# Gating the first unit alone and forming the decay between superchunks on GpSimd, in a GateLoop and GEGLU kernel

## The chip, the cores and the metric

The kernel runs on one core of a Trainium2 chip. The metric is the time of one execution on the device, in microseconds (us). Each kernel was run several times beside runs of the kernel before on the same chip. The detailed numbers come from one profiled execution of each kernel; its span is about 2 us shorter than the time that is measured for the same execution, so spans are compared with spans and times with times. A run more than 1.5% above the fastest of its kernel is called slow; ratios, their intervals and the verdicts (faster or slower from 2% on) use the other runs alone, the fast ones.

Engines in the profile: PE is TensorE (matmul), PEld its weight loads, DVE is VectorE, ACT is ScalarE, POOL is GpSimd, SP is SyncE. L239 is line 239 of that kernel's file, so the same statement can have another number in another kernel.

## The reference

A gated linear recurrence feeds a gated feed-forward layer. Sizes are 4 batches, 8 heads, 768 steps, head size 48; the second part has 3072 tokens, width 384, inner width 1536.

```python
# recurrence, for each batch and head; a is complex and |a| is capped at 0.999
for t in range(S):
    S_re, S_im = a_re*S_re - a_im*S_im + k[t] (x) v[t],  a_re*S_im + a_im*S_re
    y[t] = q[t] @ S_re
# then, on the tokens
gelu(x @ w_gate) * (x @ w_val) @ w_out      # ffn
out = x + sigmoid(x @ w_res) * ffn
```

## The kernel before

The sequence is cut into superchunks ("groups" g) of 256 steps, three to a batch. Two groups make a unit, and there are six units, 0 to 5. A unit goes through two kinds of stage:

- its gate: from `a` the log magnitude `lm` and the angle `th`; their running sums by matmul (`csl`, `cst`); `E` and `Ei`, the exponential of the sum and its inverse; an arctan; the reduction of the angle `r`, `fg`; and `CS`, the sine and cosine;
- its expert stage: the attention of the unit, with the feed-forward matmuls `gp`, `vp` and their Gelu, while the next unit's products and attention start beside it.

The first `CS` of a unit waits for the last `fg` of a group; the first Gelu of a unit comes right behind the gate of the next unit, behind a load of ScalarE's table. So the first Gelu marks the end of a gate.

The state `G` of the recurrence goes from one group to the next. It is multiplied by the decay `M` of a whole group, a product of three rows: the last row of `E` of the group before, the first row of `Ei` and the exponential of the first row of `lm`. `M` is needed with head size on partitions, and the rows have it along the free axis, so each decay goes through DRAM: rows out, then read back with another pattern (`turn`). Groups 1, 2, 4, 5, 7, 8, 10 and 11 need one: units 0, 1, 3 and 4 have one each, units 2 and 5 two each.

```python
def cs_t(g, c):                       # ... cut: angle sums into cs3 by matmul
    r = pS.tile([128, H, D], FP, tag="r", name="r")          # pS has 2 buffers of a tag
    nc.vector.tensor_scalar(out=r, in0=cs3, scalar1=MAGIC, ...)
    nc.vector.tensor_tensor(out=fg[:, hs, 1, :], in0=cs3, in1=r, op=OP.subtract)
    if c == C - 1:
        nc.vector.scalar_tensor_tensor(out=fg[:, :, 0, :], ...)       # the last fg of a group

def turn(nm, g, srcs):                # rows to DRAM (md), then back, turned (m)
    for i, src in enumerate(srcs):
        nc.gpsimd.dma_start(out=md[i:i + 1, :], in_=src)
    for u in range(2):
        nc.gpsimd.dma_start(out=m[u * D:(u + 1) * D]..., in_=md.rearrange("r (h d) -> d (r h)", h=H))
# decay0: turn the row of lm     decay1: ScalarE takes its exp, once turned
# decay2: turn the rows of E, Ei
def decay3(g):                        # two small products on VectorE
    nc.vector.tensor_tensor(out=M[0:DD], in0=m[0:DD, 0], in1=m[0:DD, 1], op=OP.mult)
    nc.vector.tensor_tensor(out=M[0:DD], in0=M[0:DD], in1=T["m1", g][0:DD, 0], op=OP.mult)

def enter():                          # in attention(g, 0), g not the first of its batch
    # s == 1:  G = dk * M        s == 2:  G = (dk + G) * M      on VectorE, then a cast to Gb

def phase_x(u):                       # gate of unit u+1, first half of the gate of u+2
    # ... cut
    weave((0.0, 0.12, csls), ..., (0.01, 0.01, dec1), (0.46, 0.46, dec),
          (0.2, 0.65, cst), (0.7, 0.95, atn + sin), (0.95, 0.95, dec3), ...)
```

`weave` gives the order in the program text. The order of instructions on each engine is then set when the kernel is compiled, by a scheduler that may move an instruction forward, and each engine runs its instructions in that order. Loads of `a`, `q`, `k` and the stores are issued on SyncE; `v`, the weights and the decay rows on GpSimd. `after_landing(t, f)` places the loads of `f` behind a small GpSimd copy of tile `t`.

Of the kernel before, what the change touches and what calls it, by code (L numbers as in the profile page):

```python
# [9 lines left out]
FP = mybir.dt.float32  # L10
BF = mybir.dt.bfloat16
AF = mybir.ActivationFunctionType
OP = mybir.AluOpType
# [3 lines left out]
def weave(*streams):  # L17

    order = []
    for si, (begin, end, steps) in enumerate(streams):  # L20
        n = len(steps)
        for i, step in enumerate(steps):
            order.append((begin + (end - begin) * (i + 0.5) / n, si, i, step))
    for _, _, _, step in sorted(order, key=lambda e: e[:3]):
        step()
# [3 lines left out]
def kernel(  # L29
# [13 lines left out]
    nc = tc.nc  # L43
    B, H, S, D = q.shape
    DD = 2 * D
    DM = H * D
# [3 lines left out]
    C = 2  # L50
    W = C * DM
    NS = S // (128 * C)
# [38 lines left out]
    pS = ctx.enter_context(tc.tile_pool(name="pS", bufs=2))  # L91
# [5 lines left out]
    mp = ctx.enter_context(tc.tile_pool(name="mp", bufs=3))  # L97
# [4 lines left out]
    dr = ctx.enter_context(tc.tile_pool(name="dr", bufs=2, space=bass.MemoryType.DRAM))  # L102
# [6 lines left out]
    T = {}  # L109
    order = mybir.DependencyInfo(mybir.DependencyClass.NoSync, mybir.DependencyReason.DATA)  # L110

    def tab(ins):

        if "tab" in T:
            tc.add_manual_dep(ins.ins, T["tab"].ins.name, order, reason="table order")
        T["tab"] = ins

    def act(**kw):
        tab(nc.scalar.activation(**kw))  # L119

    def rows(a, g, c):
        b, s = divmod(g, NS)
        t0 = (s * C + c) * 128
        return a[b, :, t0:t0 + 128, :].rearrange("h t d -> t h d")
# [9 lines left out]
    def load_q(g):  # L134
        for nm, src in (("q", q), ("k", k)):
            t = ldq.tile([128, C, H, D], FP, tag=nm, name=nm)
            for c in range(C):
                nc.sync.dma_start(out=t[:, c], in_=rows(src, g, c))
            T[nm, g] = t
        t = ldv.tile([128, C, H, D], BF, tag="v", name="v")  # L140
        for c in range(C):
            nc.gpsimd.dma_start(out=t[:, c], in_=rows(v, g, c))  # L142
        T["v", g] = t
# [15 lines left out]
    def after_landing(t, f):  # L159

        w = singles.tile([1, 1], FP, name="landed%d" % len(T))
        i = nc.gpsimd.tensor_copy(out=w, in_=t[0:1, C - 1, H - 1, D - 1:D])
        with tc.issue_after(i.ins):
            f()

    def flat(t):
        return t.rearrange("p c h d -> p (c h d)")


    def p1_steps(g):  # L170

        def s0():
            T["lm", g] = flat(T["ar", g])
            T["th", g] = flat(T["ai", g])
            act(out=T["lm", g], in_=T["lm", g], func=AF.Ln)

        def s1():
            T["s", g] = pS.tile([128, W], FP, tag="s", name="s")
            act(out=T["s", g], in_=T["lm", g], func=AF.Exp, scale=-1.0)
            nc.vector.tensor_tensor(out=T["th", g], in0=T["s", g], in1=T["th", g], op=OP.mult)  # L180

        def s2():
            act(out=T["s", g], in_=T["th", g], func=AF.Square)

        def s3():
            act(out=T["s", g], in_=T["s", g], func=AF.Ln, bias=1.0)
            lm = T["lm", g]
            nc.vector.scalar_tensor_tensor(out=lm, in0=T["s", g], scalar=0.5, in1=lm, op0=OP.mult, op1=OP.add)
            nc.vector.tensor_scalar(out=lm, in0=lm, scalar1=LNMAX, scalar2=None, op0=OP.min)  # L189

        return [s0, s1, s2, s3]
# [54 lines left out]



    def turn(nm, g, srcs):
        n = len(srcs)  # L250
        md = dr.tile([n, DM], FP, tag="d" + nm, name="d" + nm)
        for i, src in enumerate(srcs):
            nc.gpsimd.dma_start(out=md[i:i + 1, :], in_=src)
        m = mp.tile([128, n, H], FP, tag=nm, name=nm)
        for u in range(2):
            nc.gpsimd.dma_start(out=m[u * D:(u + 1) * D].rearrange("p r h -> p (r h)"),
                                in_=md.rearrange("r (h d) -> d (r h)", h=H))
        T[nm, g] = m

    def decay0(g):  # L260
        turn("m1", g, [T["lm", g][0:1, 0:DM]])

    def decay1(g):
        m = T["m1", g]
        act(out=m[0:DD], in_=m[0:DD], func=AF.Exp)

    def decay2(g):
        turn("m2", g, [T["E", g - 1][127:128, DM:W], T["Ei", g][0:1, 0:DM]])

    def decay3(g):  # L270
        m = T["m2", g]
        M = mp.tile([128, H], FP, tag="M", name="M")
        nc.vector.tensor_tensor(out=M[0:DD], in0=m[0:DD, 0], in1=m[0:DD, 1], op=OP.mult)
        nc.vector.tensor_tensor(out=M[0:DD], in0=M[0:DD], in1=T["m1", g][0:DD, 0], op=OP.mult)
        T["M", g] = M

    def products(g):
# [152 lines left out]
    def op_step(u, jj):  # L430
        h2 = T["h2", u]
        ps = psM.tile([128, DM], FP, tag="mm", padded_shape=[128, 512], name="op")
        for ffi in range(KF):
            nc.tensor.matmul(out=ps, lhsT=h2[:, ffi, jj * 128:(jj + 1) * 128], rhs=wo[:, ffi, :],  # L434
                             start=(ffi == 0), stop=(ffi == KF - 1))
        ot = ob.tile([128, DM], FP, tag="ot", name="ot")
        nc.vector.scalar_tensor_tensor(out=ot, in0=T["sg", u][:, jj], scalar=1.0, in1=ps, op0=OP.add, op1=OP.mult)  # L437
        nc.vector.tensor_tensor(out=ot, in0=ot, in1=T["x", u * 4 + jj], op=OP.add)
        t0 = (u * 4 + jj) * 128
        nc.sync.dma_start(out=out[t0:t0 + 128, :], in_=ot)  # L440


    def table(nm):
        def f():
            tab(nc.scalar.preload_act_table_set(nm))  # L445
        return f

    def gs(u):
        return [2 * u, 2 * u + 1] if 0 <= u < NU else []

    def call(f, *a):
        return lambda: f(*a)

    def zip_steps(lists):
        return [st[i] for i in range(max(map(len, lists), default=0)) for st in lists if i < len(st)]
# [12 lines left out]
    def phase_x(u):  # L468

        pend = []  # L470
        g1, g2 = gs(u + 1), gs(u + 2)
        d1 = [g for g in g1 if g % NS > 0]
        d2 = [g for g in g2 if g % NS > 0]
        ops = [call(op_step, u - 1, jj) for jj in range(4)] if 0 <= u - 1 < NU else []
        att = att_steps(u, 1)
        if not g1:
            weave((0.0, 0.8, att), (0.1, 1.0, ops))
            return

        def csl(g, c):  # L480
            pend.append(cs_l(g, c))

        def ex():
            pend.pop(0)()

        def p1(g):
            return p1_steps(g) + ([call(decay0, g)] if g % NS > 0 else [])
        csls = [call(csl, g, c) for g in g1 for c in range(C)]
        exs = [ex for _ in g1 for _ in range(C)]
        dec = [call(decay2, g) for g in d1]  # L490
        atn = [table("trig_and_small")] + [call(p1_arctan, g) for g in g2]
        cst = [call(carry, g) for g in g1] + [call(cs_t, g, c) for g in g1 for c in range(C)]
        sin = [call(p2_sin, g) for g in g1]
        dec1 = [call(decay1, g) for g in d1]
        dec3 = [call(decay3, g) for g in d1]
        table("natural_log_exp_and_others")()
        if u < 0:

            for f in [st for g in g1 for st in p1(g)] + csls + exs + dec + zip_steps([p1(g) for g in g2]) + dec1:
                f()  # L500
            for f in atn[:1] + [call(p1_arctan, g) for g in g1] + cst + sin + atn[1:] + dec3:
                f()
            return
        weave((0.0, 0.12, csls), (0.05, 0.5, zip_steps([p1(g) for g in g2])), (0.01, 0.01, dec1), (0.12, 0.45, exs),
              (0.46, 0.46, dec), (0.2, 0.65, cst), (0.7, 0.95, atn + sin), (0.95, 0.95, dec3), (0.0, 0.8, att), (0.1, 1.0, ops))

    def phase_y(u):

# [5 lines left out]
        pr = [st for g in gs(u + 1) for st in products(g)]  # L514
        weave((0.0, 1.0, gv), (0.0, 0.4, pr), (0.3, 0.95, att_steps(u + 1, 0)))

    for g in gs(0) + gs(1):
        load_a(g)
    for g in gs(0):
        load_q(g)  # L520
    after_landing(T["k", 0], load_w_in)
    for u in range(-1, NU + 1):
        phase_x(u)
        for g in gs(u + 3):
            load_a(g)
        if u == -1:
            for g in gs(1):
                load_q(g)
            after_landing(T["k", 2], load_w_out)
        phase_y(u)  # L530
        for g in gs(u + 3):
            load_q(g)


# [28 lines left out]
```

## Time and profile before

| | kernel before |
|---|---|
| time, median of 3 runs | 344.1 us (342.87 to 363.25; the longest is a slow run; a fourth run was made beside the kernel after) |
| span of the profiled run | 341.4 us |
| first CS of unit 0 | 45.46 us |
| arctan of unit 1 | 86.15 us |
| first CS of unit 1 | 88.54 us |
| decay M of unit 1 ready | 92.38 us |
| first Gelu of units 0, 1, 2, 3, 4, 5 | 95.90, 142.08, 188.52, 235.82, 279.84, 312.81 us |

Three rows of the page of the kernel before, in 40 slices of 8.5 us; a digit is a share in tenths. PE is TensorE's busy share, PEclk the granted clock, DMA the share of the DMA engines.

```profile
PE   0330544298689979899897999779999989999995
PEclk9996585559699999999999999999999999999999
DMA  9999999999999999527422620021000210002002
```

There are two regimes. Up to slice 11, about 95 us, TensorE is often idle, and its granted clock (the share of full speed that it was allowed) is at 0.5 to 0.8 in seven of the eleven slices. After that TensorE is nearly full in every second stage.

ScalarE's timeline of the kernel before (start, duration, engine, line, operation, tiles, and in brackets the idle time before it and what ended it):

```profile
45.46 0.94 ACT L119 ACTIVATE CS<-fg,hpi 128x768 bf16<-128x768 f32 x1 [7.29 <-DVE fg L237]
...
64.32 0.21 ACT L119 ACTIVATE m_268<-m_268 96x8 f32<-96x8 f32 x1 [8.90 <-DMA m_268<-dm_266]
...
86.15 1.58 ACT L119 ACTIVATE ai<-ai 128x768 f32<-128x768 f32 x2
...
88.54 0.94 ACT L119 ACTIVATE CS<-fg,hpi 128x768 bf16<-128x768 f32 x1 [0.45 <-DVE fg L237]
...
95.90 1.08 ACT L119 ACTIVATE h_776<-gp 128x512 bf16<-128x512 f32 x2
```

The chain of waits of the kernel before, the pieces of the decay (start, duration, what):

```profile
44.80 13.88 DMA dm_266<-ar
...
59.62 4.62 DMA m_268<-dm_266
...
76.31 8.40 DMA dm_663<-Ei
...
85.89 4.42 DMA m_666<-dm_663
```

A row of 1.5 KB took 13.9 us to land, and ScalarE stood 8.9 us for the turned row (`m_268`). VectorE's timeline at the end of unit 1's gate shows where the decay stood:

```profile
87.56 0.94 DVE L237 SCALAR_TENSOR_TENSOR fg<-fg 128x768 f32<-128x768 f32 x1
...
90.40 0.16 DVE L273 TENSOR_TENSOR M<-m_666 96x8 f32<-96x8 f32 x1 [0.23 <-DMA m_666<-dm_663]
...
91.35 0.95 DVE L237 SCALAR_TENSOR_TENSOR fg<-fg 128x768 f32<-128x768 f32 x1
92.22 0.16 DVE L274 TENSOR_TENSOR M<-M,m_268 96x8 f32<-96x8 f32 x1
...
93.17 0.55 DVE L344 TENSOR_TENSOR G<-G,M 96x384 f32<-96x384 f32 x1
```

The last `fg` of the gate (91.35) comes before the second product of `M` and before `G <- M`. The decay became ready late, and hardly any of the gate waited for it. Its last input (`m_666`) had landed at 90.31 us; the second product of `M` then stood behind other work of VectorE.

### The profile page before, as it was taken

The page shows a single profiled execution, that of the slowest core. Times are in us where ns is not written, and L with a number is a line of the kernel's source. Part 1 is how long each engine was busy: PE and PEld are TensorE (multiplying, and loading weights), DVE is VectorE, ACT ScalarE, POOL GpSimd, SP SyncE. Part 2 cuts the span into 40 slices and gives each one's busy share as a digit, 9 for nine tenths or more (in the row PEclk, how much of TensorE's full clock was granted, in tenths as well). Part 3 has the DMA queues.
Part 4 walks back from the last instruction along what each step waited for, and adds up shares of the span by engine and source line. Part 5 has one row for each costly group of instructions (what it writes and reads, how often), then busy time and mean ns, then how long its engine had stood idle before and what let it go on. Part 6 is the DMA issues. An engine that isn't in the chain of part 4 may idle for free.

```text
span 341.4 us, 5552 instructions
## 1 busy us (share of the span) xinstructions
PE 267.3 (78%) x2054; PEld 160.6 (47%) x2080; DVE 245.4 (72%) x440; ACT 203.0 (59%) x338; POOL 67.1 (20%) x104
## 2 busy tenths in 40 slices
PE   0330544298689979899897999779999989999995
PEld 0110224275256545465554566445665556565452
DVE  1322696249999649999389998499994799855443
ACT  3365434349665696756896656977568275662530
POOL 9423710050522224102232000150001300000000
PEclk9996585559699999999999999999999999999999
DMA  9999999999999999527422620021000210002002
GB/s 139 136 139 175 176 184 196 175 170 171 155 167 162 169 133 172 109 46 72 25 63 54 118 46 2 2 48 47 3 2 1 50 46 2 0 2 92 2 1 92
DMA packets 135258, 30.25 MB, mean 89 GB/s; under 512 B 127168, under 2 KB 135232, under 8 KB 135232
## 3 DMA queue, kind: packets, MB, share of 16 engines
q1 hardware_dynamic: 103296, 23.60, 40.6%
q0 software_dynamic: 31936, 6.31, 21.9%
q8 instruction: 16, 0.26, 0.3%
q14 instruction: 10, 0.08, 0.1%
HBM read 31.33 MB, written 4.76 MB: 106 GB/s over the span
## 4 chain that ended last, share of the span: by engine, by line
PE 47%; DMA 18%; DVE 15%; ACT 9%; issue 7%; POOL 3%; ACTq 0%; DVEq 0%; POOLq 0%
PE vp L414 12%; PE gp L410 11%; PE op L434 6%; DMA dm_266<-ar 4%; DMA v<-in_v_dram 4%; PE tp L320 3%; PE at L327 3%; PE tp L317 3%; PE rp L426 3%; DMA dm_663<-Ei 2%; ACT L445 2%; DVE fg L237 2%; DVE r L234 2%; DMA dm_219<-ar 2%; ACT CS L119 2%
## 5 line engine op out<-in xcount | busy, mean ns | idle before, releaser
L410 PE MATMUL gp<-xT,wg 128*128 128x512 bf16 x196 | 61.5, 382 | 7.6 <-DVE xT L401 4.6
L414 PE MATMUL vp<-xT,wv 128*128 128x512 bf16 x210 | 60.3, 382 | 0.3
L322 ACT COPY qk<-tp 96x512 bf16<-96x512 bf16 x48 | 27.9, 581 | 28.3 <-PE tp L320 15.1
L180 DVE TENSOR_TENSOR ai<-s,ai 128x768 f32<-128x768 f32 x12 | 11.1, 955 | 38.5 <-ACT s L119 26.9
L330 DVE TENSOR_TENSOR atm<-at,mask_81 128x512 bf16<-128x512 f32 x48 | 32.8, 683 | 7.2 <-PE at L327 7.2
L410 PEld LDWEIGHTS <-wg 128*128 128x128 bf16 x216 | 20.0, 98 | 23.0 <-issue 8.9
L317 PE MATMUL tp<-ident,Q 128*96 128x128 bf16 x192 | 20.1, 231 | 13.4 <-DVE qk L323 8.6
L142 POOL DMA_DIRECT2D v<-in_v_dram x24 | 21.3, 902 | 43.0 <-PE y L367 22.4
L414 PEld LDWEIGHTS <-wv 128*128 128x128 bf16 x216 | 20.4, 98 | 19.3 <-issue 0.8
L317 PEld LDWEIGHTS <-Q 128*96 128x96 bf16 x192 | 17.3, 131 | 21.4 <-issue 10.0
L323 DVE COPY qk<-tp 96x512 bf16<-96x512 bf16 x48 | 19.9, 414 | 10.1 <-ACT qk L322 9.6
L203 PE MATMUL csl<-ar,lt0a 128*128 128x384 f32 x24 | 12.3, 601 | 18.6 <-DVE ar L189 18.5
L119 ACT ACTIVATE CS<-fg,hpi 128x768 bf16<-128x768 f32 x12 | 11.2, 935 | 24.1 <-DVE fg L237 24.1
L445 ACT ACT_TABLE_LOAD x18 | 23.1, 1283 | 1.0 <-PEq L547 0.7
L320 PE MATMUL tp<-ident,K 128*96 128x128 bf16 x192 | 22.1, 235 | 0.0
L227 PE MATMUL cst<-ai,lt0b 128*128 128x384 f32 x24 | 11.6, 568 | 13.4 <-ACT ai L119 13.1
L327 PE MATMUL at<-qk 96*128 96x128 bf16 x192 | 20.4, 228 | 0.1
L437 DVE SCALAR_TENSOR_TENSOR ot<-sg,op 128x384 f32<-128x384 f32 x24 | 13.2, 549 | 9.4 <-PE op L434 9.4
L365 PE MATMUL y<-v,atm 128*128 128x48 bf16 x192 | 17.9, 187 | 2.5 <-DVE atm L330 2.4
L365 PEld LDWEIGHTS <-atm 128*128 128x128 bf16 x192 | 13.5, 98 | 12.8 <-DVE atm L330 11.6
L320 PEld LDWEIGHTS <-K 128*96 128x96 bf16 x192 | 17.3, 133 | 0.0
L357 PEld LDWEIGHTS <-K 128*96 128x96 bf16 x160 | 13.3, 138 | 6.5 <-DVE K L292 4.2
(155 smaller groups left out, 626.3 us busy)
## 6 DMA issues: line engine op xcount, KB each, us to landing
ar<-in_a_re_dram SPq DMA_DIRECT2D x24, 192.0 KB, 5.7
ai<-in_a_im_dram SPq DMA_DIRECT2D x24, 192.0 KB, 5.5
q<-in_q_dram SPq DMA_DIRECT2D x24, 192.0 KB, 5.1
k<-in_k_dram SPq DMA_DIRECT2D x24, 192.0 KB, 5.0
out_dram<-ot SPq DMA_DIRECT2D x24, 192.0 KB, 1.9
v<-in_v_dram POOLq DMA_DIRECT2D x24, 96.0 KB, 6.3
wg<-in_moe_w_gate_dram POOLq DMA_DIRECT2D x4, 288.0 KB, 9.2
wv<-in_moe_w_val_dram POOLq DMA_DIRECT2D x4, 288.0 KB, 10.5
```

The source lines that it names most:

```text
L142: nc.gpsimd.dma_start(out=t[:, c], in_=rows(v, g, c))
L317: nc.tensor.transpose(out=tp[0:DD, j * 128:j * 128 + 128], in_=Q(x), identity=ident)
L320: nc.tensor.transpose(out=tp[0:DD, 512 + j * 128:640 + j * 128], in_=K(x), identity=ident)
L322: nc.scalar.copy(out=qk[0:DD, 0:512], in_=tp[0:DD, 0:512])
L323: nc.vector.tensor_copy(out=qk[0:DD, 512:1024], in_=tp[0:DD, 512:1024])
L327: nc.tensor.matmul(out=at[:, j], lhsT=qk[0:DD, 512 + j * 128:640 + j * 128], rhs=qk[0:DD, j * 128:j * 128 + 128], start=True, stop=True)
L330: nc.vector.tensor_tensor(out=atm, in0=at, in1=mask4, op=OP.mult)
L365: nc.tensor.matmul(out=ys, lhsT=st["atm", hg][:, j], rhs=V(h), start=True, stop=first)
L410: nc.tensor.matmul(out=gp, lhsT=wg[:, fi, ffi * 128:(ffi + 1) * 128], rhs=xT[:, fi, :], start=(fi == 0), stop=(fi == KD - 1))
L414: nc.tensor.matmul(out=vp, lhsT=wv[:, fi, ffi * 128:(ffi + 1) * 128], rhs=xT[:, fi, :], start=(fi == 0), stop=(fi == KD - 1))
L434: nc.tensor.matmul(out=ps, lhsT=h2[:, ffi, jj * 128:(jj + 1) * 128], rhs=wo[:, ffi, :], start=(ffi == 0), stop=(ffi == KF - 1))
L445: tab(nc.scalar.preload_act_table_set(nm))
```

## The change

The intent is a faster start and a shorter decay. (1) Unit 0 is gated alone, with its q, k and v loaded ahead of unit 1's `a`; loads of v are taken out of `load_q`. (2) The row of `lm` is exponentiated before it is turned (`er`), all three rows go through DRAM in one trip, and the two products are made by GpSimd. (3) Stores are issued by GpSimd instead of SyncE. The core of the diff:

```diff
-    def turn(nm, g, srcs):            # and decay0 .. decay3: cut
+    def decay_rows(g):
+        er = pS.tile([1, DM], FP, tag="r", name="er")
+        act(out=er, in_=T["lm", g][0:1, 0:DM], func=AF.Exp)
+        md = dr.tile([3, DM], FP, tag="md", name="md")
+        for i, src in enumerate((T["E", g - 1][127:128, DM:W], T["Ei", g][0:1, 0:DM], er)):
+            nc.gpsimd.dma_start(out=md[i:i + 1, :], in_=src)
+        T["md", g] = md
+    def decay(g):
+        # ... cut: read md back, turned, into m
-        nc.vector.tensor_tensor(out=M[0:DD], in0=m[0:DD, 0], in1=m[0:DD, 1], op=OP.mult)
-        nc.vector.tensor_tensor(out=M[0:DD], in0=M[0:DD], in1=T["m1", g][0:DD, 0], op=OP.mult)
+        nc.gpsimd.tensor_tensor(out=M[0:DD], in0=m[0:DD, 0], in1=m[0:DD, 1], op=OP.mult)
+        nc.gpsimd.tensor_tensor(out=M[0:DD], in0=M[0:DD], in1=m[0:DD, 2], op=OP.mult)
 ...
-        nc.sync.dma_start(out=out[t0:t0 + 128, :], in_=ot)
+        nc.gpsimd.dma_start(out=out[t0:t0 + 128, :], in_=ot)
 ...
+        if u == 0:
+            first = [st for g in g1 for st in p1_steps(g)]
+            weave((0.0, 0.3, first), (0.3, 0.4, csls), (0.4, 0.6, exs), (0.4, 0.7, p1),
+                  (0.7, 0.75, [trig] + ...), (0.72, 0.72, dec), (0.75, 0.9, cst),
+                  (0.9, 1.0, sin + atn), (0.0, 0.8, att))
+            return
-        weave(..., (0.46, 0.46, dec), (0.2, 0.65, cst), (0.7, 0.95, atn + sin), (0.95, 0.95, dec3), ...)
+        weave((0.0, 0.12, csls), (0.05, 0.5, p1), (0.12, 0.45, exs), (0.46, 0.46, dec), (0.2, 0.65, cst),
+              (0.7, 0.95, [trig] + atn + sin), (0.0, 0.8, att), (0.1, 1.0, ops))
 ...
-    for g in gs(0) + gs(1):
+    for g in gs(0):
         load_a(g)
     for g in gs(0):
         load_q(g)
-    after_landing(T["k", 0], load_w_in)
+        load_v(g)
+    for g in gs(1):
+        load_a(g)
+    after_landing(T["ai", 2], load_w_in)
+    for g in gs(1):
+        load_q(g)
     # ... in the loop over u, behind phase_x(-1):
-            after_landing(T["k", 2], load_w_out)
+            after_landing(T["q", 2], lambda: [load_v(g) for g in gs(1)])
+            after_landing(T["q", 3], load_w_out)
```

In the program text the products of `M` move from mark 0.95 of a phase to 0.72 (unit 1) or 0.46 (later units), ahead of part or all of the `cst` steps which end in `fg`.

More of the change, by code (lines that the diff above doesn't have):

```diff
@@ L139, in load_q, with load_v @@
             T[nm, g] = t
+    def load_v(g):
         t = ldv.tile([128, C, H, D], BF, tag="v", name="v")
@@ L245, in p2_sin @@
         act(out=T["CS", g][:, :, 1], in_=T["fg", g][:, :, 1], func=AF.Sin, scale=2.0 * math.pi)
-    def turn(nm, g, srcs):
-        n = len(srcs)
-        md = dr.tile([n, DM], FP, tag="d" + nm, name="d" + nm)
-        for i, src in enumerate(srcs):
+    def decay_rows(g):
[3 more added lines that the diff above has]
+        for i, src in enumerate((T["E", g - 1][127:128, DM:W], T["Ei", g][0:1, 0:DM], er)):
             nc.gpsimd.dma_start(out=md[i:i + 1, :], in_=src)
-        m = mp.tile([128, n, H], FP, tag=nm, name=nm)
+        T["md", g] = md
+    def decay(g):
+        m = mp.tile([128, 3, H], FP, tag="m", name="m")
         for u in range(2):
             nc.gpsimd.dma_start(out=m[u * D:(u + 1) * D].rearrange("p r h -> p (r h)"),
-                                in_=md.rearrange("r (h d) -> d (r h)", h=H))
-        T[nm, g] = m
-    def decay0(g):
-        turn("m1", g, [T["lm", g][0:1, 0:DM]])
-    def decay1(g):
-        m = T["m1", g]
-        act(out=m[0:DD], in_=m[0:DD], func=AF.Exp)
-    def decay2(g):
-        turn("m2", g, [T["E", g - 1][127:128, DM:W], T["Ei", g][0:1, 0:DM]])
-    def decay3(g):
-        m = T["m2", g]
+                                in_=T["md", g].rearrange("r (h d) -> d (r h)", h=H))
         M = mp.tile([128, H], FP, tag="M", name="M")
-        nc.vector.tensor_tensor(out=M[0:DD], in0=m[0:DD, 0], in1=m[0:DD, 1], op=OP.mult)
-        nc.vector.tensor_tensor(out=M[0:DD], in0=M[0:DD], in1=T["m1", g][0:DD, 0], op=OP.mult)
+        nc.gpsimd.tensor_tensor(out=M[0:DD], in0=m[0:DD, 0], in1=m[0:DD, 1], op=OP.mult)
+        nc.gpsimd.tensor_tensor(out=M[0:DD], in0=M[0:DD], in1=m[0:DD, 2], op=OP.mult)
         T["M", g] = M
@@ L472, in phase_x @@
         d1 = [g for g in g1 if g % NS > 0]
-        d2 = [g for g in g2 if g % NS > 0]
         ops = [call(op_step, u - 1, jj) for jj in range(4)] if 0 <= u - 1 < NU else []
@@ L484, in ex @@
             pend.pop(0)()
-        def p1(g):
-            return p1_steps(g) + ([call(decay0, g)] if g % NS > 0 else [])
         csls = [call(csl, g, c) for g in g1 for c in range(C)]
-        exs = [ex for _ in g1 for _ in range(C)]
-        dec = [call(decay2, g) for g in d1]
-        atn = [table("trig_and_small")] + [call(p1_arctan, g) for g in g2]
+        exs = [ex for _ in g1 for _ in range(C)] + [call(decay_rows, g) for g in d1]
+        dec = [call(decay, g) for g in d1]
         cst = [call(carry, g) for g in g1] + [call(cs_t, g, c) for g in g1 for c in range(C)]
         sin = [call(p2_sin, g) for g in g1]
-        dec1 = [call(decay1, g) for g in d1]
-        dec3 = [call(decay3, g) for g in d1]
+        trig = table("trig_and_small")
         table("natural_log_exp_and_others")()
         if u < 0:
-            for f in [st for g in g1 for st in p1(g)] + csls + exs + dec + zip_steps([p1(g) for g in g2]) + dec1:
-                f()
-            for f in atn[:1] + [call(p1_arctan, g) for g in g1] + cst + sin + atn[1:] + dec3:
+            for f in ([st for g in g1 for st in p1_steps(g)] + csls + exs + [trig]
+                      + [call(p1_arctan, g) for g in g1] + dec + cst + sin):
                 f()
             return
-        weave((0.0, 0.12, csls), (0.05, 0.5, zip_steps([p1(g) for g in g2])), (0.01, 0.01, dec1), (0.12, 0.45, exs),
-              (0.46, 0.46, dec), (0.2, 0.65, cst), (0.7, 0.95, atn + sin), (0.95, 0.95, dec3), (0.0, 0.8, att), (0.1, 1.0, ops))
+        atn = [call(p1_arctan, g) for g in g2]
+        p1 = zip_steps([p1_steps(g) for g in g2])
+        if u == 0:
+            first = [st for g in g1 for st in p1_steps(g)]
+            weave((0.0, 0.3, first), (0.3, 0.4, csls), (0.4, 0.6, exs), (0.4, 0.7, p1),
+                  (0.7, 0.75, [trig] + [call(p1_arctan, g) for g in g1]), (0.72, 0.72, dec), (0.75, 0.9, cst),
+                  (0.9, 1.0, sin + atn), (0.0, 0.8, att))
+            return
+        weave((0.0, 0.12, csls), (0.05, 0.5, p1), (0.12, 0.45, exs), (0.46, 0.46, dec), (0.2, 0.65, cst),
+              (0.7, 0.95, [trig] + atn + sin), (0.0, 0.8, att), (0.1, 1.0, ops))
     def phase_y(u):
@@ L526 @@
         if u == -1:
-            for g in gs(1):
-                load_q(g)
-            after_landing(T["k", 2], load_w_out)
+            after_landing(T["q", 2], lambda: [load_v(g) for g in gs(1)])
+            after_landing(T["q", 3], load_w_out)
         phase_y(u)
@@ L532 @@
             load_q(g)
+            load_v(g)
 _INS = ['q', 'k', 'v', 'a_re', 'a_im', 'moe_w_gate', 'moe_w_val', 'moe_w_out', 'moe_w_res']
```

## The prediction

> **What bounds the kernel now.** Two regimes. From the first Gelu at 95.9 us (timeline of ScalarE) to the end, 245 us: alternating stages of about 23 us (gates: ScalarE 19 to 20 us busy, VectorE 18) and 24 us (expert: TensorE 22.6 to 23.8 busy), in the table by windows. Before 95.9 us TensorE is busy 41 us only. The 40 slices show the DMA engines full until about 145 us. The chain of waits there is made of DMA: v (8.4 us), dm_219 (6.9), dm_266 (13.9), m_268 (4.6), dm_663 (8.4), m_666 (4.4), the last four being the decay's trips through DRAM.
>
> **What the change does.**
> 1. Early part. Only 4 of 12 v loads come first, and q/k of unit 0 precede a of unit 1. At the measured 150 GB/s, a of unit 0 has landed at 14.5 us instead of 17, a of unit 1 at 35. ScalarE no longer stands still for m_268 (8.9 us) or for unit 1's gate: the first CS should come near 33 us instead of 45.5, attention of unit 0 12 us earlier.
> 2. But unit 0's expert stage waits for unit 1's gate and for a of unit 2, which now lands behind q/k of unit 1: 40 SyncE loads (7.9 MB), at 0.075 MB/us beside the weights and 0.10 beside v (read from the windows): near 70 us, against 65 before.
> 3. The order of instructions (compiled) puts 7 v loads, 3 wo and 5 v loads on GpSimd between w_in and unit 1's decay. Trainium skill, "DMA: Bandwidth & Descriptors", Queues, rings and completion order: each DMA engine consumes a ring in order. This trace agrees: dm_266, issued 2 us behind wr, landed 0.4 us behind it, 13.9 us after issue. So unit 1's md rows wait: w_in from 33 us takes 21.5 us (36.8 to 58.3 before), 7 v 15 us (12 took 26), wo 10, 5 v 11: exp'd row landed near 89. Then m (5 us), two GpSimd products (0.5), and VectorE, whose order now has G <- M before all r and fg of unit 1, where before M came after most; also er shares r's two buffers, so an r waits for that landing too. From M to the first Gelu: G, fg, two CS, arctan, table, about 13 us. First Gelu near 109 us, 13 later than before.
> 4. Later units: no m exps or M on ScalarE and VectorE (0.7 us per unit, off the chain), but G <- M now stands amid fg where DMA hops of 2 to 3 us each end later: +3 us in unit 2's gate, about +1 in two others, estimates. Stores leave SyncE, whose waits cost nothing; at the end a GpSimd issue adds perhaps 0.5.
>
> Sum: 344 - 0 + 13 + 5 = 362; shaded toward before for a wrong ring model: 359 us, 80% range 346 to 371. Chances: faster by over 2% 0.06, within 2% 0.16, slower 0.78.
>
> **What would show it.** Timeline: first CS near 33 us (step 1); first Gelu near 109 (steps 2, 3); unit 1's md<-er landing near 89, with GpSimd held at md by earlier DMA (step 3); waits of VectorE G on GpSimd M, 10 us or more in unit 1, some us later (steps 3, 4). From first Gelu to the end about 250 us against 245.
>
> **What would make it wrong.** If the GpSimd ring drains faster than it did here (v loads 2.2 us each beside SyncE traffic), md lands before 78 us and the first Gelu comes near 91 to 95: then 340 to 345. If GpSimd is held longer by stores waiting for VectorE, later gates lose more than 5 us. If the expert stages were limited by SyncE stores mixed with loads, which the trace doesn't show, the change would gain there.

## More of the kernel before

Times from one first Gelu to the next measure a whole unit.

`enter` and the other steps of the attention are traced under `tc.high_priority()`, in both kernels.

## The result, and the profile after

| | before | after |
|---|---|---|
| time, median | 344.96 us (342.87 to 363.25, 4 runs) | 367.96 us (365.29 to 370.28, 4 runs) |
| ratio of fast runs | | 1.0686, 95% interval 1.0576 to 1.0796: slower |
| span | 341.4 us | 363.2 us |
| first CS of unit 0 | 45.46 us | 31.29 us |
| arctan of unit 1 | 86.15 us | 76.94 us |
| M of unit 1 ready | 92.38 us | 94.29 us |
| first CS of unit 1 | 88.54 us | 98.74 us |
| first Gelu, units 0, 1, 2 | 95.90, 142.08, 188.52 us | 107.94, 159.38, 206.13 us |
| first Gelu, units 3, 4, 5 | 235.82, 279.84, 312.81 us | 254.98, 300.09, 333.20 us |

A ratio is the mean time of one kernel's fast runs over the mean of the other's fast runs of the same rounds; so it isn't quite the ratio of the medians quoted beside it, and the slow run of 363.25 us isn't in it.

ScalarE's timeline after, the lines that answer to those before:

```profile
31.29 0.94 ACT L119 ACTIVATE CS<-fg,hpi 128x768 bf16<-128x768 f32 x1 [6.30 <-DVE fg L239]
...
76.94 1.58 ACT L119 ACTIVATE ai<-ai 128x768 f32<-128x768 f32 x2
98.74 0.94 ACT L119 ACTIVATE CS<-fg,hpi 128x768 bf16<-128x768 f32 x1 [20.22 <-DVE fg L239]
...
107.94 1.09 ACT L119 ACTIVATE h_762<-gp 128x512 bf16<-128x512 f32 x2
```

The start did get faster, 14 us at the first CS and 9 us at unit 1's arctan. Then ScalarE stood 20.2 us for an `fg`. VectorE's timeline after tells why:

```profile
78.42 0.56 DVE L219 TENSOR_TENSOR P<-P 128x384 f32<-128x384 f32 x1
94.32 0.55 DVE L336 TENSOR_TENSOR G<-G,M 96x384 f32<-96x384 f32 x1 [15.35 <-POOL M L266]
94.91 0.35 DVE L338 CAST Gb<-G 96x384 bf16<-96x384 f32 x1
95.18 0.55 DVE L236 TENSOR_SCALAR r<-cst 128x384 f32<-128x384 f32 x1
...
97.76 0.95 DVE L239 SCALAR_TENSOR_TENSOR fg<-fg 128x768 f32<-128x768 f32 x1
```

`G <- M` now stands ahead of every `r` and `fg` of unit 1's gate. It waited 15.35 us for `M`, and the gate waited behind it. `M` itself came only 1.9 us later than before (94.29 against 92.38 us), its last input 3.4 us later (93.67 against 90.31).

Where `M` was is told by GpSimd's timeline after and by the chain of waits after (two fences):

```profile
71.90 0.52 POOL L256 DMA_DIRECT2D md<-Ei  x1 [2.13 <-DMA wo<-in_moe_w_out_dram]
74.53 0.52 POOL L256 DMA_DIRECT2D md<-E  x1 [2.10 <-ACT xT L391]
77.61 0.49 POOL L256 DMA_DIRECT2D md<-er  x1 [2.56 <-DMA wo<-in_moe_w_out_dram]
87.75 1.75 POOL L262 DMA_DIRECT2D m<-md  x2 [9.65 <-DMA md<-er]
93.81 0.19 POOL L265 TENSOR_TENSOR M<-m 96x8 f32<-96x8 f32 x1 [4.31 <-DMA m<-md]
```

```profile
43.19 16.14 DMA v<-in_v_dram
59.61 17.08 DMA wo<-in_moe_w_out_dram
...
77.61 9.56 DMA md<-er
...
88.66 5.01 DMA m<-md
```

`er` was formed on ScalarE at 69.67 us, but GpSimd came to its transfer at 77.61, behind 12 loads of v and three of wo, and the transfer then took 9.56 us.

The cost is seen in the table by windows (length, then busy time and instructions of PE, PEld, DVE, ACT and POOL, granted clock, DMA share, which can pass 1 in this view, and GB/s). The stretch from 77 to 95 us, first before, then after:

```profile
77.00:95.00 18.00, 13.23 (x90) 7.17 (x88) 17.50 (x31) 15.30 (x24) 5.48 (x8) 0.81 1.40 164
```

```profile
77.00:95.00 18.00, 5.82 (x12) 2.95 (x12) 2.46 (x6) 1.52 (x2) 2.60 (x5) 0.69 1.29 158
```

VectorE (third) was busy 17.5 of 18 us before and 2.5 after. All compute engines stood for most of it.

The difference of the first Gelus (after minus before) is 12.0, 17.3, 17.6, 19.2, 20.3 and 20.4 us for units 0 to 5, and 21.8 at the end. So 12.0 us are lost before the first Gelu, 5.3 in unit 2's gate, then 0.3, 1.5, 1.1 and 0.1, and 1.4 at the very end. Unit 2's gate has the same picture on VectorE:

```profile
151.88 0.55 DVE L333 TENSOR_TENSOR G<-dk,M 96x384 f32<-96x384 f32 x1 [4.74 <-POOL M L266]
```

In the kernel before, this instruction came behind the gate's last `fg` (138.12) and waited for nothing:

```profile
141.36 0.55 DVE L341 TENSOR_TENSOR G<-dk,M 96x384 f32<-96x384 f32 x1
```

### The profile page after: what moved, and what is told of

It is laid out like the page before. It is cut to its first block, busy times and chain, and to the rows that moved or that the text cites. A ratio compares the mean times of both kernels' runs of the same rounds, so it can differ in the third digit from the quotient of the medians.

```text
span 363.2 us, 5540 instructions
## 1 busy us (share of the span) xinstructions
PE 275.4 (76%) x2080; PEld 165.7 (46%) x2080; DVE 245.8 (68%) x424; ACT 206.1 (57%) x338; POOL 75.7 (21%) x129
## 4 chain that ended last, share of the span: by engine, by line
PE 45%; DMA 23%; DVE 10%; ACT 9%; issue 8%; POOL 4%; SPq 1%; POOLq 0%; ACTq 0%; DVEq 0%
PE gp L402 12%; PE vp L406 12%; DMA m<-md 5%; DMA wo<-in_moe_w_out_dram 5%; DMA v<-in_v_dram 4%; DMA md<-er 4%; PE op L426 4%; PE rp L418 3%; PE tp L312 3%; PE at L319 2%; DMA wg<-in_moe_w_gate_dram 2%; PE tp L309 2%; ACT s L119 2%; DMA ar<-in_a_re_dram 2%; POOL m L262 2%
## 5 line engine op out<-in xcount | busy, mean ns | idle before, releaser
L402 PE MATMUL gp<-xT,wg 128*128 128x512 bf16 x216 | 65.2, 388 | 14.6 <-DVE fg L237 12.8
L406 PE MATMUL vp<-xT,wv 128*128 128x512 bf16 x216 | 64.4, 386 | 0.0
L402 PEld LDWEIGHTS <-wg 128*128 128x128 bf16 x216 | 20.3, 99 | 32.6 <-issue 16.4
L432 POOL DMA_DIRECT2D out_dram<-ot x24 | 13.5, 564 | 76.3 <-DVE ot L430 68.6
L406 PEld LDWEIGHTS <-wv 128*128 128x128 bf16 x216 | 20.3, 98 | 17.8 <-issue 1.1
L309 PEld LDWEIGHTS <-Q 128*96 128x96 bf16 x192 | 18.4, 136 | 14.9 <-DVE Q L284 5.9
L312 PE MATMUL tp<-ident,K 128*96 128x128 bf16 x192 | 22.9, 241 | 0.0
L429 DVE SCALAR_TENSOR_TENSOR ot<-sg,op 128x384 f32<-128x384 f32 x24 | 13.2, 549 | 10.7 <-PE op L426 10.7
L357 PE MATMUL y<-v,atm 128*128 128x48 bf16 x192 | 17.5, 190 | 2.6 <-DVE atm L322 1.6
L256 POOL DMA_DIRECT2D md<-Ei x8 | 4.1, 507 | 72.8 <-ACT Ei L119 70.7
## 6 DMA issues: line engine op xcount, KB each, us to landing
wg<-in_moe_w_gate_dram POOLq DMA_DIRECT2D x4, 288.0 KB, 10.2
```

Of the source, the lines that this page charges most:

```text
L309: nc.tensor.transpose(out=tp[0:DD, j * 128:j * 128 + 128], in_=Q(x), identity=ident)
L312: nc.tensor.transpose(out=tp[0:DD, 512 + j * 128:640 + j * 128], in_=K(x), identity=ident)
L357: nc.tensor.matmul(out=ys, lhsT=st["atm", hg][:, j], rhs=V(h), start=True, stop=first)
L402: nc.tensor.matmul(out=gp, lhsT=wg[:, fi, ffi * 128:(ffi + 1) * 128], rhs=xT[:, fi, :], start=(fi == 0), stop=(fi == KD - 1))
L406: nc.tensor.matmul(out=vp, lhsT=wv[:, fi, ffi * 128:(ffi + 1) * 128], rhs=xT[:, fi, :], start=(fi == 0), stop=(fi == KD - 1))
```

## The experiments

The theory after the result: the loss needs two things at once. `M` comes late because its rows queue on GpSimd behind bulk loads and then make two trips through DRAM; and `G <- M` stands ahead of the gate's `fg` in VectorE's fixed order, so that a late `M` holds the gate. Rivals: `a` of unit 2, now loaded behind q and k of unit 1, comes too late; the stores on GpSimd disturb; the products are slow on GpSimd.

All runs below gave correct results. They were made in three batches, each on one chip (the first four experiments, the next four, the last four); ratios are to the kernel before in the same batch.

### Decay rows ahead of the bulk loads (decay_first)

The output weights and the v of units 2 and 3 are issued behind unit 1's `M`, in the kernel after.

```diff
-        nc.gpsimd.tensor_tensor(out=M[0:DD], in0=M[0:DD], in1=m[0:DD, 2], op=OP.mult)
+        T["Mi", g] = nc.gpsimd.tensor_tensor(out=M[0:DD], in0=M[0:DD], in1=m[0:DD, 2], op=OP.mult).ins
 ...
-            after_landing(T["q", 3], load_w_out)
+        if u == 0:
+            with tc.issue_after(T["Mi", 2]):
+                load_w_out()
+                for g in gs(2): load_v(g)
         phase_y(u)
         for g in gs(u + 3):
             load_q(g)
-            load_v(g)
+            if u == 0:
+                with tc.issue_after(T["Mi", 2]): load_v(g)
+            elif u > 0: load_v(g)
```

> The changed kernel, with only the order of GpSimd's loads altered: the wo load and the v loads of units 2 and 3 are issued behind unit 1's decay product M instead of ahead of its md rows. Theory (unit 1's decay rows stand in GpSimd's ring behind 8 v loads and 3 wo loads, and VectorE's G <- M holds the fg of the same stage): md<-er lands near 75 us instead of 87.2, VectorE's wait for M before G (15.3 us in the changed kernel) falls to about 3 us, first Gelu near 94 to 96 us instead of 107.9, total 352 to 355 us against 367. Rival (a of unit 2 lands later because q/k are loaded before it): no change, under 3 us.

Measured: 358.06 us (357.4 to 360.15), ratio 1.0423 (1.0379 to 1.0467). VectorE's timeline of it:

```profile
83.95 0.55 DVE L336 TENSOR_TENSOR G<-G,M 96x384 f32<-96x384 f32 x1 [5.60 <-POOL M L266]
```

`M` was ready at 83.91 us, 10.4 us earlier; first Gelu at 97.73, 10.2 us earlier. The row `er` was issued at 72.73 instead of 77.61, and from there to the start of the products it took 10.7 us (to 83.44) instead of 16.2 (to 93.81). So the bulk ahead of it cost 4.9 us of issue and 5.5 us of transfer. Even so, `G` waited 5.60 us and unit 2's gate 5.50 us: the second half of the theory is still there.

### G behind the last fg (g_late)

The kernel after, with `er` in a buffer of its own and every `G <- M` issued behind the last `fg` that the program has traced by then.

```diff
-        er = pS.tile([1, DM], FP, tag="r", name="er")
+        er = pS.tile([1, DM], FP, tag="er", name="er")
 ...
-            nc.vector.scalar_tensor_tensor(out=fg[:, :, 0, :], ...)
+            T["fgi"] = nc.vector.scalar_tensor_tensor(out=fg[:, :, 0, :], ...).ins
 ...
-        return [hi(f) for f in (enter, grp(0), dk, grp(1), yy)]
+        def enter_late():
+            with tc.issue_after(T["fgi"]):
+                enter()
+        return [hi(f) for f in (enter_late, grp(0), dk, grp(1), yy)]
```

> The changed kernel, GpSimd's order left as it is, but VectorE's G <- M is issued behind the last fg of the stage, and the row er has a buffer of its own instead of sharing r's two. Theory: the late M no longer holds fg; first CS of unit 1 near 83 us instead of 98.7; the first Gelu moves from 107.9 to about 98 (attention of unit 1 still waits for M at 94); unit 2's gate loses about 4.5 us of wait, two later gates 1 to 2 us each; total 350 to 354 us. If the late M matters by its attention and not by fg, the total stays within 3 us of 367.

Measured: 355.11 us (353.34 to 356.4), ratio 1.0323 (1.0276 to 1.0371). `M` was no earlier (ready at 95.91 us), but the first CS of unit 1 came at 88.13 instead of 98.74 and the first Gelu at 100.02 instead of 107.94. The waits of `G` for `M` in unit 1 and unit 2 were 3.0 and 2.3 us instead of 15.3 and 4.7, and unit 1's first Gelu came 49.6 us after unit 0's instead of 51.4. So with `G` behind `fg` about 13 us are gone, with `M` as late as ever. VectorE's timeline of it:

```profile
90.71 0.95 DVE L239 SCALAR_TENSOR_TENSOR fg<-fg 128x768 f32<-128x768 f32 x1
...
95.95 0.55 DVE L336 TENSOR_TENSOR G<-G,M 96x384 f32<-96x384 f32 x1 [2.96 <-POOL M L266]
```

The run isn't pure: it also holds the `G` of a unit's second group, whose last traced `fg` belongs to the next gate, and it changes the buffer. The later runs trace the last `fg` of the unit's own gate.

### a of unit 2 ahead of q and k of unit 1 (a2_first)

```diff
+    for g in gs(2):
+        load_a(g)
     for g in gs(1):
         load_q(g)
 ...
-            load_a(g)
+            if u >= 0: load_a(g)
 ...
-            after_landing(T["q", 2], lambda: [load_v(g) for g in gs(1)])
-            after_landing(T["q", 3], load_w_out)
+            after_landing(T["ar", 4], lambda: [load_v(g) for g in gs(1)])
+            after_landing(T["ar", 5], load_w_out)
```

> The changed kernel, with a of unit 2 loaded by SyncE before q/k of unit 1 instead of after; GpSimd's order as it is, its two gates moved to the loads that now stand in the same places. Rival (the expert stage of unit 0 waits for a of unit 2): Ln of the second half of unit 2 at about 55 us instead of 64.5, first Gelu 9 us earlier, total near 358. Theory (it waits for the decay of unit 1): Ln earlier by as much, but M stays at 94 us and the first Gelu at 107 to 109; total within 2 us of 367.

Measured: 368.57 us (367.21 to 368.95), ratio 1.0708 (1.0664 to 1.0752), so nothing gained. The arctan of unit 1 came at 68.69 us, 8 us earlier, and `G` waited 24.61 us instead of 15.35: `M` at 95.30, first Gelu at 109.01. The earlier gate was all turned into waiting. The late `a` isn't the cause of the loss.

### Stores back on SyncE (stores_sync)

```diff
-        nc.gpsimd.dma_start(out=out[t0:t0 + 128, :], in_=ot)
+        nc.sync.dma_start(out=out[t0:t0 + 128, :], in_=ot)
```

> The changed kernel with the stores back on SyncE. Rival (stores on GpSimd hold its decay work back): most of the 23 us comes back. Theory: the first Gelu stays at 108 us; 1 to 2 us less at the end of the span (4.1 us from the last VectorE instruction to the end, 2.7 before), 1 to 2 us less in unit 2's gate, where a store stands between the md row and m; total 363 to 366 us.

Measured: 364.25 us (363.43 to 365.61), ratio 1.0596 (1.0555 to 1.0638). First Gelu at 107.91 us, as in the kernel after. The stores are worth some 3 us by this run, which is not clear of noise (the interval overlaps that of the kernel after, 1.0576 to 1.0796), and they are not the loss. The run on the kernel before (before_stores_gp, below) tells what they cost.

### Products on VectorE (m_vector)

```diff
-        nc.gpsimd.tensor_tensor(out=M[0:DD], ...)      # both products
+        nc.vector.tensor_tensor(out=M[0:DD], ...)
```

> The changed kernel with the two decay products back on VectorE; everything else as changed. Rival (GpSimd forms M too slowly, or its products collide with VectorE): 5 us or more come back. Theory (the products cost 0.2 us each and it is the row's way through the GpSimd ring and the place of G <- M in VectorE's order that cost): the compiled VectorE order still has M and G ahead of all r and fg of unit 1, so the first Gelu stays at 107 to 109 us and the total within 3 us of 367.

Measured: 369.03 us (368.26 to 370.19), ratio 1.0731 (1.0686 to 1.0775). VectorE's first product of unit 1 stood 7.75 us for `m`, and `G` followed at 94.52 us, still ahead of all `fg`. In the kernel after GpSimd had taken 0.19 and 0.20 us for them. (Elsewhere it took longer, 2.31 and 1.39 us at 133.6 us of mended_plain_er, beside a VectorE without a gap; why isn't shown.) The engine that makes the products isn't the cause; nor does bringing them back to VectorE bring back the old order.

### The decay part alone, in the kernel before (before_decay)

`decay_rows` and `decay` as in the diff above put into the kernel before; load order, stores and `u == 0` branch are left as they were.

```diff
-        exs = [ex for _ in g1 for _ in range(C)]
-        dec = [call(decay2, g) for g in d1]
-        # decay0, decay1, decay3 and their places in the weaves: cut
+        exs = [ex for _ in g1 for _ in range(C)] + [call(decay_rows, g) for g in d1]
+        dec = [call(decay, g) for g in d1]
```

> The kernel before, with only the decay taken from the change (row exp'd on ScalarE, all three rows through one DRAM tile, products on GpSimd); its load order, its stages and its stores on SyncE stay. Theory: ScalarE no longer waits for m_268, but unit 1's row is now formed late and stands behind wo and two v loads, so the first Gelu stays near 96 us (93 to 99); G <- M stands amid fg again, so unit 2's gate loses about 5 us and two later gates 1 to 1.5 us each: 348 to 353 us against 343.7. Rival (the whole loss is in the load order and the stages of unit 0, the decay is a gain by itself): 335 to 343 us.

Measured: 358.75 us (358.12 to 359.72), ratio 1.0432 (1.039 to 1.0473). I had expected 348 to 353; the cost was 14.4 us between the medians. VectorE's timeline:

```profile
93.59 0.56 DVE L334 TENSOR_TENSOR G<-G,M 96x384 f32<-96x384 f32 x1 [6.45 <-POOL M L264]
94.07 0.55 DVE L235 TENSOR_TENSOR fg<-cst,r 128x384 f32<-128x384 f32 x1
```

Here `M` was ready at 93.56 us, 1.2 us later than in the kernel before, and no load order had been touched; yet `G` stood ahead of three of unit 1's `fg`, and the second CS of the unit came at 96.51 instead of 92.33, the first Gelu at 100.01 instead of 95.90. The waits of `G` for `M` sum to 13.8 us over the run (7.4 in one line, 6.4 in the other). So the decay part costs 14.4 of the 23.0 us between the medians of the kernels before and after, and doesn't need the new load order for that. But only 4.1 us of it lie before the first Gelu, where the kernel after loses 12.0, and 6.5 in unit 2's gate (5.3 there): most of what the kernel after loses before its first Gelu comes only together with the new order of loads and stages, and decay_first got 10.2 us of it back by moving loads alone.

### er sent at once (er_early)

The kernel after, with `er` formed as soon as `lm` is there, in its own buffer, and sent ahead of the two other rows.

```diff
+    def decay_er(g):
+        er = pS.tile([1, DM], FP, tag="er", name="er")
+        act(out=er, in_=T["lm", g][0:1, 0:DM], func=AF.Exp)
+        nc.gpsimd.dma_start(out=md[2:3, :], in_=er)       # allocation of md moved here
     def decay_rows(g):
-        ...                                               # three rows
+        ...                                               # the two others only
 ...
+        weave((0.0, 0.3, first), (0.3, 0.3, ers), ...)    # and mark 0.0 in later units
```

> The changed kernel, with the row exp(lm) formed and sent as soon as lm is there (at the start of the stage for units 2 on) instead of after the eight exps, and in a buffer of its own. GpSimd's v and wo loads stay ahead of unit 1's rows. Theory: the late row is what makes VectorE wait for M in unit 2's gate (4.7 us): first Gelu of unit 0 to that of unit 1 falls from 51.4 us to 46 to 48; the first Gelu itself stays at 107 to 110, because unit 1's rows still queue behind v and wo; total 360 to 363 us. If the wait in unit 2's gate comes from the DMA hops alone, the 51.4 us stay.

Measured: 374.22 us (373.07 to 374.93), ratio 1.087 (1.0817 to 1.0923): the slowest of all, where I had expected 360 to 363. `er` was issued 9.6 us earlier (67.97 us), but `M` was ready no earlier (94.47), since the row of `Ei`, issued at 74.98, now was the late one: GpSimd waited 12.51 us for it. And the compiled order put `G` still further forward, ahead of some `lm` work of unit 2 as well: `G` waited 16.45 us and the first Gelu came at 114.48. Speeding one input of the decay changed the order to the worse and the landing not at all.

### Four repairs without the place of G (mended)

decay_first, a2_first, er_early and stores_sync together (with `load_v` of unit 1 behind `ar` of unit 2).

> The changed kernel with every suspected cost taken out together: wo and v of units 2 and 3 behind unit 1's M, row exp(lm) early and in its own buffer, a of unit 2 loaded before q/k of unit 1, stores on SyncE. Theory: M of unit 1 near 69 us, no long wait before G, first Gelu 85 to 90 us (95.9 in the kernel before, 107.9 in the changed one), first Gelu to first Gelu of the next unit 46 to 48 us, total 334 to 341 us, under both kernels. If something else in the unit-0-alone stage costs the time, the total stays above 350.

Measured: 352.69 us (352.24 to 354.33), ratio 1.0262 (1.0217 to 1.0306); I had expected 334 to 341. The arctan of unit 1 ran at 68.73 us and `M` came at 73.76, 20.5 us earlier than in the kernel after. VectorE's timeline:

```profile
73.79 0.56 DVE L340 TENSOR_TENSOR G<-G,M 96x384 f32<-96x384 f32 x1 [9.10 <-POOL M L270]
```

`G` moved forward with it, and still waited 9.1 us, with unit 2's `lm` work, `P`, `r` and `fg` of unit 1 behind it: first CS of unit 1 at 85.43, first Gelu at 94.69. Unit 2's gate lost 4.0 us to the same wait (50.3 us from first Gelu to first Gelu). A decay that comes 20.5 us earlier brought the first Gelu 13.3 us forward and the time 15.3 us down, but not under the kernel before: `G` is placed just as far ahead of it. The next runs test whether that is what is left.

### The four repairs with G behind fg (mended_g_late and mended_plain_er)

mended_g_late is mended with `G` held behind the last `fg` of the unit's own gate; mended_plain_er is the same without er_early (three rows together, own buffer for `er`).

```diff
+        T["fgx"] = T["fgi"]                   # behind each phase_x
 ...
+        def enter_late():
+            with tc.issue_after(T["fgx"]):
+                enter()
```

> The mended kernel (q/k of unit 1 behind a of unit 2, output weights and later v behind unit 1's M, er sent early, stores on SyncE) with one thing more: every unit's G <- M is held in VectorE's order behind the last fg of that unit's gate. Theory (the loss needs a late M and a G that stands ahead of fg): the wait of 9.1 us of G on M before unit 2's lm work and the one of 4.0 us in unit 2's gate are gone from the chain; first CS near 77 to 80 us (mended: 85.4), first Gelu near 86 to 89 (94.7), the next ones 46 to 48 us apart (50.3 in mended); time 334 to 341 us, under the kernel before (344). Rival (the early part is limited by the arrival of a and q/k, and the place of G only decides which wait is seen): first Gelu stays above 93 and the time at 349 to 353.

> As mended_g_late, but er is formed and sent with the other two rows, as in the changed kernel (own buffer for it). Theory: with G behind fg the decay has time until about 78 to 80 us; unit 1's M comes at 78 to 83, so G waits 0 to 4 us and nothing that the gate needs stands behind it: within 3 us of mended_g_late. Rival (sending er early is needed): M above 85 us and 5 us or more slower than mended_g_late.

Measured: mended_g_late 342.22 us (340.67 to 342.89), ratio 0.9959 (0.9908 to 1.001). VectorE's timeline of it:

```profile
80.43 0.95 DVE L239 SCALAR_TENSOR_TENSOR fg<-fg 128x768 f32<-128x768 f32 x1
...
82.64 0.55 DVE L340 TENSOR_TENSOR G<-G,M 96x384 f32<-96x384 f32 x1
```

No `G` waited for `M` any more, the first CS of unit 1 came at 77.86 us and the first Gelu at 86.83, 7.9 us earlier than in mended and within the band on record; the interval to the next is 47.9 us instead of 50.3. So the place of `G` is worth 10.5 us between the medians of two kernels whose text differs in it alone (the medians are of two batches, with the kernel before at 344.33 and 344.44). The total missed the band by 1.2 us: the next two intervals from first Gelu to first Gelu were 49.7 and 48.4 us, longer than the 46 to 48 that I expected.

mended_plain_er 338.02 us (337.36 to 339.94), ratio 0.9862 (0.9801 to 0.9923): it beats both kernels, by 1.4% or some 4.7 us against the kernel before (6.4 between the medians, with a slow run of the kernel before, 347.55, among them) and by 29.9 against the median of the kernel after (of another batch). That is under the 2% at which a kernel is called faster here, but the interval leaves 1 out. It is 4.2 us faster than mended_g_late, where I had expected them within 3 us; the same two intervals are 47.7 and 46.6 us here, so the early `er` costs in later units; by what way stays open. VectorE's timeline of mended_plain_er:

```profile
79.58 0.95 DVE L239 SCALAR_TENSOR_TENSOR fg<-fg 128x768 f32<-128x768 f32 x1
80.45 0.55 DVE L335 TENSOR_TENSOR G<-dk,G 96x384 f32<-96x384 f32 x1
...
81.78 0.55 DVE L336 TENSOR_TENSOR G<-G,M 96x384 f32<-96x384 f32 x1
```

`M` was ready at 76.13 us, before `G` was reached, and nothing waited in unit 1; in unit 2's gate `G` waited 1.4 us. The first Gelu came at 86.27 us, 9.6 us before that of the kernel before; the span is 6.1 us shorter, so some 3.5 us were given back in later units.

### The decay part with G behind fg, in the kernel before (before_decay_g_late)

before_decay, with `er` in its own buffer and `enter_late` as above.

> The kernel before with the decay part alone, as in before_decay (358.8 us), but er in a buffer of its own and every G <- M held behind the last fg of its gate. Theory: the decay part costs its 14 us because G stands ahead of fg while M is late; with G behind fg, first Gelu back within 2 us of 96 and the next ones 46 to 47 us apart; time 343 to 349. Rival (the decay part costs by the longer chain of its transfers, or by its products on GpSimd, wherever G stands): 355 to 360.

Measured: 347.02 us (346.84 to 348.89), ratio 1.0117 (1.0066 to 1.0169), within the band. 11.7 of before_decay's 358.75 us are gone, with `M` ready at 94.04 us, no earlier than the 93.56 there. VectorE's timeline:

```profile
87.49 0.95 DVE L237 SCALAR_TENSOR_TENSOR fg<-fg 128x768 f32<-128x768 f32 x1
...
94.07 0.56 DVE L334 TENSOR_TENSOR G<-G,M 96x384 f32<-96x384 f32 x1 [4.30 <-POOL M L264]
```

The detail came out otherwise than expected: the first Gelu is at 91.45 us, 4.5 earlier than in the kernel before, and the next one 53.0 us later instead of 46 to 47. `G` with its wait of 4.3 us now stands ahead of `K` and of the expert stage's own vector work, so what the gate no longer waits for, the expert stage does. The wait moved to a place where it costs less; the 2.6 us that remain between the medians (4.0 by the ratio) fit that, but no run shows their place. The run changes two things, the buffer of `er` and the place of `G`; in before_decay an `r` waited 1.6 us for the `er` row's landing, ahead of a `G` that waited anyway, so I put little on the buffer, but no run separates it.

### The stores alone, in the kernel before (before_stores_gp)

```diff
-        nc.sync.dma_start(out=out[t0:t0 + 128, :], in_=ot)
+        nc.gpsimd.dma_start(out=out[t0:t0 + 128, :], in_=ot)
```

> The kernel before with the stores issued by GpSimd alone. From stores_sync (364.3 against 368.0 for the whole change, bands almost touching): 344 to 348, at most 4 us above the kernel before, by the tail (2.7 us from the last VectorE instruction to the end, 4.1 with GpSimd stores) and nothing in the first Gelu (95.9). Rival (the stores delay the decay rows and v on GpSimd's queue): later Gelus more than 1 us further apart per unit and 350 or more.

Measured: 347.24 us (346.15 to 348.1), ratio 1.011 (1.0061 to 1.0159). First Gelu at 97.32 us (95.90 before), the end of the last vector instruction at 340.43 us (338.66), the span 346.3 (341.4). So of 4.9 us between the spans 3.1 lie behind the last vector instruction: 5.87 us from there to the end instead of 2.74. In the kernel after it is 4.15 us, and in stores_sync 2.75.

## Why the prediction was right

The prediction said slower by over 2% with a chance of 0.78, and 359 us, 346 to 371. The kernel took 367.96 us. Point by point:

- Step 1, the earlier start: right. First CS predicted near 33 us, measured 31.29. Predicted to be worth nothing in the end, and it was: unit 1's arctan was 9.2 us earlier, and `G` waited it away.
- Step 2, `a` of unit 2 near 70 us: right. VectorE went on from its landing at 71.95. It isn't what limited (a2_first).
- Step 3, the decay rows behind GpSimd's loads and `G` ahead of `fg`: right in mechanism and size. The `er` row was predicted to land near 89 us, and landed at 87.2; first Gelu predicted near 109, measured 107.94; wait of `G` for `M` at least 10 us, measured 15.35. The base of this was the Trainium skill, "DMA: Bandwidth & Descriptors", section Queues, rings and completion order, by which each DMA engine consumes a ring's descriptors in order. (The page says this of the rings that SyncE and ScalarE use, and adds there that transfers need not complete in that order; that GpSimd's transfers queue alike was read from the trace.) decay_first agrees: with the bulk no longer ahead, the way from the issue of `er` to the products took 10.7 us instead of 16.2. It shows the effect of queueing behind GpSimd's loads; it doesn't separate the ring from the total load on the DMA engines, because the bulk was moved behind and not taken away.
- What the prediction left in one term: "13 later than before" is the first Gelu, not `M`. Its own steps put `M` at about 94.5 us (89, 5 and 0.5), measured 94.29, and 13 us from there to the first Gelu, measured 13.65; it didn't say how late `M` had been before, 92.38. So the 12 us do not come from a later `M`, which is 1.9 us. They come from two things together: the place of `G`, which makes the gate wait for `M` at all, and an `M` that is as late as ever although the gate is ready 9 us sooner. In before_decay, where the gate's arctan is only 3.2 us sooner (82.98 against 86.15) and `M` 1.2 us later, 4.1 us are lost before the first Gelu. The prediction named the place of `G` ("where before M came after most"), but gave it no size of its own; mended against mended_g_late does, 10.5 us.
- The buffer that `er` shares with `r`, also named in step 3, cost nothing here: no `r` of the kernel after waited for `er` (one waited 1.6 us in before_decay).
- Step 4: right in kind, too small. "+3 us in unit 2's gate" measured 5.3; "about +1 in two others" measured 0.3, 1.5, 1.1 and 0.1; "perhaps 0.5" at the end measured 1.4 (4.15 us against 2.74 behind the last vector instruction). The time from first Gelu to the end was predicted as about 250 us against 245, and measured 255.3 against 245.5.
- The shading from the sum of 362 to 359 us "for a wrong ring model" went the wrong way; the terms of step 4 were the ones to widen.
- Rivals: late `a`, the stores as a main cause, and slow products are each refuted by a run. The stores' own cost is 2.8 us between the medians in the kernel before and 3.7 in the kernel after, the latter not clear of noise.

What stays open: why the scheduler places `G` so far ahead. The products of `M` stand earlier in the program text than before, which would do it, and their return to VectorE alone (m_vector) didn't undo it; no run moved them alone to the old mark. `enter` stands under `tc.high_priority()` in both kernels, so that a `G` whose `M` is traced earlier may be moved far forward; no run took it off. Open too are the share of each of the three other repairs in mended_plain_er, and the 3.5 us that it gives back in later units.

## What to carry to other kernels

An instruction that depends on a slow side path (a trip through DRAM, another engine's queue) belongs in the in-order stream of its engine behind everything that doesn't need it: look in the compiled order for its place and hold it back explicitly before making the side path faster, since a faster side path alone got back only part of the 23.0 us here (9.9 in decay_first, 15.3 in mended with its other repairs) or lost time (er_early). A small transfer that the next stage needs should not be issued on a queue behind bulk loads. An earlier start is a gain only if what ends last there, here the decay, comes earlier too or is moved out of the way.

## What the Trainium skill lacked or had wrong

- "DMA: Bandwidth & Descriptors", section Anatomy of one DMA: its fit for a GpSimd-issued DMA, a fixed part of about 2.0 us plus bytes over bandwidth, gives about 2.0 us for a row of 1.5 KB (an estimate from that page). In the kernel after the transfers that write or read `md` (1.5 to 4.5 KB) took 1.5 us at least, 3.0 in the median and 14.9 at most from issue to landing (in the median 1.8, 2.9 and 2.6 us for the rows of `E`, `Ei` and `er`, 4.0 for the turned read), and the `er` row of unit 1 9.56. The page has no figure for a small transfer behind bulk on the same queue.
- "DMA: Bandwidth & Descriptors", section Specifications: it gives a first byte after about 1 us on the GpSimd path and 0.6 us on the SyncE path. From the last vector instruction to the end, with the last store between them, 2.74 and 2.75 us were measured with SyncE and 4.15 and 5.87 us with GpSimd, so the difference was 1.4 to 3.1 us, where these two figures differ by 0.4. Issue and completion are in these numbers, which the page's first byte isn't meant to cover.
- "TensorE: Matmul & The Clock Gate", Part 1: The HAM clock gate, has the PE array start slow and become fast about 4 us into sustained matmuls. The trace of the kernel after agrees: the first pair of 128x384 fp32 `cst` matmuls after an idle time of 11.21 us, at 77.84, took 1.65 us, and the pairs from 81.56 on, 3.7 us later, 0.81. Nothing was lacking here.
- No page was found that gives a size for what an instruction's place in an engine's fixed order can cost: 10.5 us here, between mended and mended_g_late.
